# Chunked mLSTM with a gated MLP on one core: the state's part of the values computed in 64x64 tiles of the array, with the state and the scaled queries split by head half

## The chip, the cores and the metric

The kernel runs on one core of a Trainium2 chip. The metric is the device time of one execution in microseconds (us), taken as the median of several runs. The engines go by the profile's names: PE is the matrix unit (its weight loads are listed apart as PEld), DVE the vector engine, ACT the scalar engine, POOL the general-purpose engine, SP the queue that issues most transfers.

## The reference

A gated linear recurrence runs over 768 time steps for 4 x 8 = 32 batch-head pairs with head size 40; its output is regrouped into 3072 tokens of 320 features, and a two-layer MLP with a gate follows.

```python
for t in range(S):
    m_new = np.maximum(f_gate[:, :, t] + m, i_gate[:, :, t])
    f_stab = np.exp(f_gate[:, :, t] + m - m_new)
    i_stab = np.exp(i_gate[:, :, t] - m_new)
    C = f_stab[..., None, None] * C + i_stab[..., None, None] * einsum('bhd,bhe->bhde', vt, kt)
    n = f_stab[..., None] * n + i_stab[..., None] * kt
    h_tilde = einsum('bhde,bhe->bhd', C, qt);  denom = max(abs(n . qt), 1)
    y[:, :, t] = sigmoid(o_gate) * h_tilde / denom
x = y as (3072, 320)
h = x @ w_in;  g = h * sigmoid(h);  out = g @ w_out
```

## The kernel before

**Units.** The recurrence is computed in chunks of 64 steps (12 chunks, index c). The 32 batch-head pairs form two groups (index p) of 16 sequences. One chunk of one group is a unit, n = 2c + p, 24 in all. The 16 sequences of a unit are ordered by two batch halves and 8 heads; the code splits the 8 into two halves of four. In the kernel's indices d and a each stand for a half: a tile's rows hold one half (rows 0-39 and rows 64-103), its columns the other.

**What a unit does.** `scores` (L516) multiplies keys and queries in 64x64 tiles of the array. `weigh` (L550) multiplies the scores by the decay matrix `D`. `near_values` (L587) multiplies the weighted scores with the values of the same chunk, also in 64x64 tiles: 16 matmuls, four to a round over two row halves d and two column halves g. `far_values` (L604) adds what comes from the state of all chunks before: 8 matmuls that use all 104 rows of the scaled queries `qt` against the state `Cm`, whose tile holds two columns blocks per row, one of them zero (82 columns in all). `state` (L660) forms this chunk's contribution `pu`. `carry` (L677) decays the state on POOL (L688, by the last column of `lq`) and adds `pu` on DVE (L694). The scaled queries come from `near` (L506), one POOL multiplication of `q` and `lq`, 104 rows by 512, behind `look` (L503), the exponential of `lq` on ACT. The first three units use `values` (L566) in place of `near_values` and `far_values`.

**The MLP.** Three units give 384 tokens, a step j (8 steps). A step runs through 16 column blocks fc of the hidden layer: `mm1` (L763) makes `ph`, `act` makes `g` with ACT (L770) and DVE (L776 in step 0, L784 and L793 later), `mm2` (L814) adds the block of two fc earlier to the output. Steps after the first split each operand in a high and a low part and so take more matmuls.

**What sets the order.** All engines run orders written out by hand: the order of the calls. In step j the three units of step j + 1 are woven in. `PLACES` (L41) says at which fc each unit's block starts: 5, 9 and 12 in step 0 and 2, 7 and 12 later. At that fc `block` (L845) issues, behind `mm1`, the scores of the next unit, then `near_values`, `far_values` and `state` of this one. Two fc later (`2 in at`, L1062) `misc` of the next unit issues `look` on ACT and `near` on POOL. Unit 5, the last of the three woven into step 0, so has its `near` at fc 11 and its block at fc 12; all later units have two fc or more between them. Unit 5's output is normed and scaled by DVE behind the block (`norm`, `level`, `scale`), and `carry` follows.

PE works through its instructions in the order written; a matmul that waits holds back all behind it. The pair tile `p` has 8 heads x 128 columns: the scores in columns 0 to 63 of each head, the values from column 64 on. Every POOL or ACT instruction waits its turn in the same way. `qt`, `lq` have two buffers each.

Of the kernel before, what the change touches and what calls it, by code (L numbers as in the profile page):

```python
# [8 lines left out]
F32 = mybir.dt.float32  # L9
# [5 lines left out]
ALU = mybir.AluOpType  # L15
# [3 lines left out]
B, H, S, D = 4, 8, 768, 40  # L19
L = 64  # L20
NC = S // L
NP = B // 2
# [4 lines left out]
UPS = 3  # L27
# [3 lines left out]
D1 = D + 1  # L31
DA = 32
HD1 = H * D1
KS = 64 + D
# [9 lines left out]
def mlstm_mlp_kernel(  # L44
# [12 lines left out]
    nc = tc.nc  # L57
    pool = lambda n, b, **kw: ctx.enter_context(tc.tile_pool(name=n, bufs=b, **kw))
    cp = pool("cp", 1)
    p2 = pool("p2", 2)  # L60
# [19 lines left out]
    for k in range(2):  # L80
        m = mask[k * L : (k + 1) * L]
        nc.gpsimd.affine_select(
            out=m, in_=m, compare_op=ALU.is_ge, fill=NEG, base=0,
# [253 lines left out]
        nmade[0] = min(nmade[0] + n, len(parts))  # L337


    Cm = [cp.tile([KS, 2, HD1], F32, name=f"Cm{p}") for p in range(NP)]  # L340
    vb = [cp.tile([128, 2, HD1], F32, name=f"vb{k}") for k in range(3)]
    for t in vb:
        for k in range(2):
            nc.gpsimd.memset(t[k * L : (k + 1) * L, 1 - k, :], 0.0)
    for t in Cm:
        nc.gpsimd.memset(t, 0.0)

    def bank(n, pool_, tag, shape, name):

        if n < UPS:  # L350
            return pool_.tile(shape, F32, tag=tag, name=name)
        return psU.tile(shape, F32, tag="u", name=name)
# [5 lines left out]
    class Unit:  # L358
# [62 lines left out]
        def reach_act(self):  # L421
            self.lq = p2.tile([128, H, L], F32, tag="lq", name=f"lq{self.n}")
            nc.scalar.activation(self.lq[:KS], self.eq[:KS], AF.Exp)

        def load_d(self):
            n, c, p = self.n, self.c, self.p
            self.Dm = p3.tile([128, H, L], F32, tag="D", name=f"D{n}")
            for k in range(2):
                r = p * 2 * H + k * H
                nc.sync.dma_start(  # L430
                    self.Dm[k * L : (k + 1) * L],
                    LFd[c, r : r + H, :].unsqueeze(0).broadcast_to([L, H, L]),
                )
# [68 lines left out]

        def look(self):  # L503
            nc.scalar.activation(self.lq[:KS], self.lq[:KS], AF.Exp)  # L504

        def near(self):  # L506
            self.qt = p2.tile([KS, H, L], F32, tag="qt", name=f"qt{self.n}")
            nc.gpsimd.tensor_tensor(out=self.qt, in0=self.q[:KS], in1=self.lq[:KS], op=ALU.mult)  # L508

        def misc(self):  # L510
# [55 lines left out]
        def values(self):  # L566

            p, po = self.p, self.out
            ops = [(po[:, :, a, e, :], self.Dm, self.vt, a, e) for a in range(2) for e in range(2)]
            if self.c > 0:  # L570
                ops += [
                    (po[:, d, :, e, :], self.qt, Cm[p].rearrange("p a (h f) -> p a h f", f=D1), d, e)
                    for d in range(2)
                    for e in range(2)
                ]
            for i, (to, w, m, x, e) in enumerate(ops):
                for g in range(2):
                    j = x * 4 + e * 2 + g
                    nc.tensor.matmul(
                        to[g * L : (g + 1) * L],  # L580
                        w[:, j, :],
                        m[:, :, j, :],
                        start=(i == 0),
                        stop=(i == len(ops) - 1),
                    )
# [16 lines left out]
                            )  # L602

        def far_values(self):  # L604
            cm = Cm[self.p].rearrange("p a (h f) -> p a h f", f=D1)
            for d in range(2):
                for e in range(2):
                    for g in range(2):
                        j = d * 4 + e * 2 + g
                        nc.tensor.matmul(  # L610
                            self.out[g * L : (g + 1) * L, d, :, e, :],
                            self.qt[:, j, :],
                            cm[:, :, j, :],
                            start=False,
                            stop=True,
                            skip_group_check=True,
                        )

        def norm(self):
            n, po = self.n, self.po  # L620
# [39 lines left out]
        def state(self):  # L660
            n, c, p = self.n, self.c, self.p
            if c == NC - 1:
                return
            pu = bank(n, psO, "o", [128, H, D1], f"pu{n}")
            by_d = pu.rearrange("p (d j) f -> p j d f", d=2)
            for j in range(4):
                for a in range(2):
                    nc.tensor.matmul(  # L668
                        by_d[a * 64 : a * 64 + D, j],
                        self.kw[:, a * 4 + j, :],  # L670
                        self.vt[:, :, a * 4 + j, :],
                        start=True,
                        stop=True,
                    )
            self.pu = pu

        def carry(self, copy=nc.scalar.copy):  # L677
            n, c, p = self.n, self.c, self.p
            if c == NC - 1:
                return  # L680
            pu = self.pu
            for a in range(2):
                r = slice(a * 64, a * 64 + D)
                v = Cm[p][r, a, :].rearrange("p (h e) -> p h e", e=D1)
                if c == 0:
                    copy(v, pu[r])
                    continue
                nc.gpsimd.tensor_tensor(  # L688
                    out=v,
                    in0=v,  # L690
                    in1=self.lq[r, :, L - 1].unsqueeze(2).broadcast_to([D, H, D1]),
                    op=ALU.mult,
                )
                nc.vector.tensor_tensor(out=v, in0=v, in1=pu[r], op=ALU.add)  # L694

        def room(self, to=psH, tag="h"):
            n = self.n
# [210 lines left out]
    for _ in range(2):  # L908
        nc.tensor.matmul(
            dummy, ident, ident.unsqueeze(1).broadcast_to([128, 4, 128]), start=True, stop=True  # L910
        )
    two = gates(2 * L, 4 * L)
    near, far = spread(2 * L, 4 * L, nc.gpsimd), spread(4 * L, S, nc.gpsimd)
    late = [gates(4 * L, 8 * L), gates(8 * L, S)]
    widen()
# [75 lines left out]
            u2.carry(),  # L991
            run(5, two),
            run(1, near),
            u3.reach_act(),
        ),
# [3 lines left out]
            u3.weigh(),  # L999
            wmake(2),  # L1000
            run(2, near),
            u4.load_kvo(),
            u4.load_d(),
# [152 lines left out]
```

## Time and profile before

| what | value |
|---|---|
| median of 3 runs | 448.28 us (447.94 to 448.96) |
| the profiled execution's own time | 447.96 us |
| its span, first to last instruction | 446.2 us |
| ACT busy | 209.7 us (47%) |
| DVE busy | 270.8 us (61%) |
| POOL busy | 123.1 us (28%) |
| granted PE clock | 1.000 |

The page gives each engine's busy time, the chain of work that ended last and the costliest groups of instructions; the views of waits, of the chain by time and of the timeline in a window are answers of the same trace. A duration in the timeline is that of one instruction or, with "x16", of a run of them from the first start to the last end. Matmuls overlap, so what a stage costs PE is read from ends or starts of successive stages, never from the sum of durations. One fp32 matmul leaves two records: the 16 matmuls of `near_values` stand as x32, the 8 of `far_values` as x16.

### The profile page before, as it was taken

Reading aid. Unit: us, or ns where it says so; the run is one execution under the profiler, and the core shown is the slowest. Engines: PE = TensorE matmul, PEld = TensorE weight load, DVE = VectorE, ACT = ScalarE, POOL = GpSimd, SP = SyncE. Lnnn points to the kernel's source line nnn. Section 1 sums busy time; section 2 is a strip of 40 time slices with the busy share of each in tenths; the row PEclk is TensorE's granted clock in tenths of the full one; section 3 lists DMA queues with packets and bytes.
Section 4 is the critical chain, followed back from the end, with each engine's and each line's share of the span. In section 5 each row is a group of like instructions: output and inputs, shape, how many; then the busy total and the mean of one; then the engine's idle time right before and its main releaser. Section 6 shows DMA issues by size and latency. Waiting matters only on the chain.

```text
span 446.2 us, 11064 instructions
## 1 busy us (share of the span) xinstructions
PE 439.0 (98%) x4488; PEld 406.1 (91%) x4488; DVE 270.8 (61%) x595; ACT 209.7 (47%) x439; POOL 123.1 (28%) x134
## 2 busy tenths in 40 slices
PE   8899999999999999999999999999999999999996
PEld 4667667899999999999999999999999999999995
DVE  5888699477874664654664656646646555444442
ACT  7683956445745434435435344354344354334332
POOL 5834144133231431431341323314314220000000
PEclk9999999999999999999999999999999999999999
DMA  8999695251340631424421433406314100001001
GB/s 259 379 355 311 182 298 148 82 166 41 119 140 23 163 111 34 137 53 133 141 86 55 126 82 118 140 18 170 100 42 141 46 25 1 1 1 46 0 1 44
DMA packets 28691, 50.38 MB, mean 113 GB/s; under 512 B 3968, under 2 KB 15248, under 8 KB 28640
## 3 DMA queue, kind: packets, MB, share of 16 engines
q1 hardware_dynamic: 28288, 49.25, 36.2%
q8 instruction: 35, 0.57, 0.5%
q10 hardware_dynamic: 288, 0.34, 0.3%
q14 instruction: 16, 0.13, 0.1%
q0 software_dynamic: 64, 0.08, 0.1%
HBM read 45.65 MB, written 4.01 MB: 111 GB/s over the span
## 4 chain that ended last, share of the span: by engine, by line
PE 95%; DMA 3%; SPq 1%; ACT 1%; DVE 0%; issue 0%
PE ph L763 42%; PE pout L814 40%; PE p L610 3%; PE p L524 3%; PE pu L668 3%; PE p L595 2%; PE p L710 2%; DMA qk<-in_qk_dram 1%; DMA ko<-in_ko_dram 1%; PE pt L195 1%; SPq L459 0%; DVE wi L257 0%; SPq L439 0%; SPq L450 0%; ACT wri L255 0%
## 5 line engine op out<-in xcount | busy, mean ns | idle before, releaser
L770 ACT ACTIVATE th<-ph 128x384 f32<-128x384 f32 x128 | 62.4, 487 | 156.0 <-PE ph L763 154.9
L784 DVE SCALAR_TENSOR_TENSOR th<-th,ph 128x384 f32<-128x384 f32 x112 | 62.2, 555 | 89.2 <-ACT th L770 88.5
L763 PE MATMUL ph<-xh,wh 128*128 128x384 f32 x336 | 115.3, 343 | 0.0
L763 PE MATMUL ph<-xl,wh 128*128 128x384 f32 x336 | 113.7, 338 | 0.0
L814 PE MATMUL pout<-woh,gh 128*128 128x320 f32 x336 | 105.4, 314 | 0.0
L814 PE MATMUL pout<-woh,gl 128*128 128x320 f32 x336 | 103.9, 309 | 0.0
L814 PE MATMUL pout<-wol,gh 128*128 128x320 f32 x336 | 103.2, 307 | 0.0
L793 DVE TENSOR_TENSOR gl<-th,gh 128x384 fp32r<-128x384 f32 x112 | 65.6, 586 | 47.5 <-ACT gh L789 47.5
L789 ACT CAST gh<-th 128x384 fp32r<-128x384 f32 x112 | 57.5, 513 | 63.4 <-DVE th L784 62.8
L763 PE MATMUL ph<-xh,wl 128*128 128x384 f32 x224 | 75.9, 339 | 0.0
L814 PEld LDWEIGHTS pout<-woh,gh 128*128 128x128 f32 x336 | 63.0, 188 | 2.0
L763 PEld LDWEIGHTS ph<-xh,wh 128*128 128x128 f32 x336 | 63.1, 188 | 0.2
L763 PEld LDWEIGHTS ph<-xl,wh 128*128 128x128 f32 x336 | 63.1, 188 | 0.2
L814 PEld LDWEIGHTS pout<-woh,gl 128*128 128x128 f32 x336 | 63.0, 188 | 0.1
L814 PEld LDWEIGHTS pout<-wol,gh 128*128 128x128 f32 x336 | 63.1, 188 | 0.0
L688 POOL TENSOR_TENSOR Cm<-Cm,lq 40x328 f32<-40x328 f32 x40 | 30.4, 761 | 117.8 <-PE p L610 116.2
L508 POOL TENSOR_TENSOR qt<-qk,lq 104x512 f32<-104x512 f32 x22 | 28.9, 1314 | 121.6 <-ACT lq L504 109.0
L763 PEld LDWEIGHTS ph<-xh,wl 128*128 128x128 f32 x224 | 42.1, 188 | 0.0
L814 PE MATMUL pout<-wo,g 128*128 128x320 f32 x96 | 28.7, 435 | 0.0
L491 POOL TENSOR_TENSOR D<-D,am 128x512 f32<-128x512 f32 x20 | 25.8, 1290 | 4.8 <-DMA D<-LFd 3.3
L483 POOL TENSOR_TENSOR am<-mask,aT 128x512 f32<-128x512 f32 x20 | 24.1, 1206 | 6.6 <-DVE aT L205 5.2
L763 PE MATMUL ph<-x,wi 128*128 128x384 f32 x64 | 23.6, 492 | 1.3 <-DVE wi L257 1.3
(120 smaller groups left out, 488.1 us busy)
## 6 DMA issues: line engine op xcount, KB each, us to landing
qk<-in_qk_dram SPq DMA_DIRECT2D x24, 512.0 KB, 5.1
ko<-in_ko_dram SPq DMA_DIRECT2D x24, 320.0 KB, 4.7
wro<-in_w_out_dram SPq DMA_DIRECT2D x8, 640.0 KB, 7.2
D<-LFd SPq DMA_DIRECT2D x40, 128.0 KB, 3.4
lq<-LFd SPq DMA_DIRECT2D x40, 128.0 KB, 4.2
wri<-in_w_in_dram SPq DMA_DIRECT2D x8, 512.0 KB, 6.8
vb<-in_vp_dram SPq DMA_DIRECT2D x48, 82.0 KB, 4.6
out_dram<-ob SPq DMA_DIRECT2D x45, 80.0 KB, 2.1
```

What stands on the lines that cost most here:

```text
L483: nc.gpsimd.tensor_tensor(out=self.am, in0=mask.unsqueeze(1).broadcast_to([128, H, L]), in1=aT[:, self.c, self.p, :].unsqueeze(2).broadcas ...
L491: nc.gpsimd.tensor_tensor(out=self.Dm, in0=self.Dm, in1=self.am, op=ALU.add)
L508: nc.gpsimd.tensor_tensor(out=self.qt, in0=self.q[:KS], in1=self.lq[:KS], op=ALU.mult)
L524: nc.tensor.matmul(self.ps[d * L : (d + 1) * L, a * 4 + j, :], self.k[r, d * 4 + j, :], self.q[r, d * 4 + j, :], start=True, stop=True,)
L610: nc.tensor.matmul(self.out[g * L : (g + 1) * L, d, :, e, :], self.qt[:, j, :], cm[:, :, j, :], start=False, stop=True, skip_group_check=True,
L688: nc.gpsimd.tensor_tensor(out=v, in0=v, in1=self.lq[r, :, L - 1].unsqueeze(2).broadcast_to([D, H, D1]), op=ALU.mult,)
L763: nc.tensor.matmul(ph, w, x, start=(i == 0), stop=(i == len(ops) - 1))
L770: nc.scalar.activation(th, ph, AF.Tanh, scale=0.5)
L784: nc.vector.scalar_tensor_tensor(out=th, in0=th, scalar=1.0, in1=ph, op0=ALU.add, op1=ALU.mult)
L789: nc.scalar.copy(gh, th)
L793: nc.vector.tensor_tensor(out=gl, in0=th, in1=gh.bitcast(F32), op=ALU.subtract)
L814: nc.tensor.matmul(self.po[t], g[:, ts], w, start=(fc == 0 and i == 0), stop=(last and i == len(ops) - 1),)
```

## The change

The state is now kept with one head half on rows 0-39 and the other on rows 64-103, without the zero blocks (328 columns in place of 2 x 328). `far_values` issues 16 matmuls of 40 rows and 41 columns, in the same order of halves as `near_values`, in place of 8 matmuls of 104 rows and 82 columns. The scaled queries have to stand in the same layout, so `near` writes them in four quarters (40 rows by 256), two of which go from one row half to the other. The decay of the state has to stand there too: `decay` copies the last column of `lq` to a new tile `fl` in four small ACT copies behind `look`. `carry` decays with `fl` (still two POOL instructions of 40 by 328) and adds `pu` in four DVE instructions of 40 by 164 in place of two of 40 by 328. The first three units keep the old layout in `C0` and write the new one at their end; in the opening ACT and DVE copy or add the state in quarters too, and POOL clears one state tile in place of two.

```diff
-    Cm = [cp.tile([KS, 2, HD1], F32, name=f"Cm{p}") for p in range(NP)]
+    Cm = [cp.tile([KS, HD1], F32, name=f"Cm{p}") for p in range(NP)]
+    C0 = cp.tile([KS, 2, HD1], F32, name="C0")
...
-    for t in Cm:
-        nc.gpsimd.memset(t, 0.0)
+    nc.gpsimd.memset(C0, 0.0)
...
+        def decay(self):
+            if self.n < UPS:
+                return
+            self.fl = p2.tile([128, H], F32, tag="fl", name=f"fl{self.n}")
+            for d, a, r, w in self.turns():
+                nc.scalar.copy(self.fl[w, a * 4 : a * 4 + 4], self.lq[r, d * 4 : d * 4 + 4, L - 1])
+        @staticmethod
+        def turns():
+            rows = [slice(x * 64, x * 64 + D) for x in range(2)]
+            return [(d, a, rows[a], rows[d]) for d in range(2) for a in range(2)]
...
         def look(self):
             nc.scalar.activation(self.lq[:KS], self.lq[:KS], AF.Exp)
+            self.decay()
...
         def near(self):
             self.qt = p2.tile([KS, H, L], F32, tag="qt", name=f"qt{self.n}")
+            if self.n >= UPS:
+                for d, a, r, w in self.turns():
+                    nc.gpsimd.tensor_tensor(
+                        out=self.qt[w, a * 4 : a * 4 + 4, :],
+                        in0=self.q[r, d * 4 : d * 4 + 4, :],
+                        in1=self.lq[r, d * 4 : d * 4 + 4, :],
+                        op=ALU.mult,
+                    )
+                return
             nc.gpsimd.tensor_tensor(out=self.qt, in0=self.q[:KS], in1=self.lq[:KS], op=ALU.mult)
...
         def far_values(self):
-            cm = Cm[self.p].rearrange("p a (h f) -> p a h f", f=D1)
-            for d in range(2):
+            cm = Cm[self.p].rearrange("p (h f) -> p h f", f=D1)
+            for a in range(2):
                 for e in range(2):
-                    for g in range(2):
-                        j = d * 4 + e * 2 + g
-                        nc.tensor.matmul(
-                            self.out[g * L : (g + 1) * L, d, :, e, :],
-                            self.qt[:, j, :],
-                            cm[:, :, j, :],
...
+                    for d in range(2):
+                        r = slice(d * 64, d * 64 + D)
+                        for g in range(2):
+                            j = a * 4 + e * 2 + g
+                            nc.tensor.matmul(
+                                self.out[g * L : (g + 1) * L, d, a, e, :],
+                                self.qt[r, j, :],
+                                cm[r, j, :],
...
         def carry(self, copy=nc.scalar.copy):
...
+            for d in range(2):
+                w = slice(d * 64, d * 64 + D)
                 nc.gpsimd.tensor_tensor(
-                    out=v,
-                    in0=v,
-                    in1=self.lq[r, :, L - 1].unsqueeze(2).broadcast_to([D, H, D1]),
+                    out=new[w],
+                    in0=new[w],
+                    in1=self.fl[w].unsqueeze(2).broadcast_to([D, H, D1]),
                     op=ALU.mult,
                 )
-                nc.vector.tensor_tensor(out=v, in0=v, in1=pu[r], op=ALU.add)
+                for a in range(2):
+                    v = new[w, a * 4 : a * 4 + 4, :]
+                    nc.vector.tensor_tensor(
+                        out=v, in0=v, in1=self.pu[d][a * 64 : a * 64 + D], op=ALU.add
+                    )
```

Two places show how the instructions move. The first is PE at fc 12 of step 0, the block of unit 5 (p6 is the pair tile, D5 the weighted scores of unit 5, Cm1 the state of its group, qt5 its scaled queries). Before:

```order
L595 MATMUL p6_1035<-vb2_137,D5_690 64x41 [waits DMAHW7_49,DMAHW2_49]
L595 MATMUL p6_1035<-vb2_137,D5_690 64x41
L595 MATMUL p6_1035<-vb2_137,D5_690 64x41 [waits DMAHW3_49,DMAHW0_49]
L595 MATMUL p6_1035<-vb2_137,D5_690 64x41 x13
L610 MATMUL p6_1035<-Cm1_134,qt5_1009 64x2x41 [waits Pool_49]
L610 MATMUL p6_1035<-Cm1_134,qt5_1009 64x2x41 x7
L668 MATMUL pu5_1076<-vb2_137,kw5_845 40x2x41 x8
L814 MATMUL pout0_0_582<-wo5_990,g0_10_970 128x320 [waits DVE_49]
```

And with the change, from the last matmuls of `near_values` (now L621) on:

```order
L621 MATMUL p6_1085<-vb2_138,D5_704 64x41 x13
L639 MATMUL p6_1085<-Cm1_134,qt5_1056 64x41 [waits Pool_49]
L639 MATMUL p6_1085<-Cm1_134,qt5_1056 64x41
L639 MATMUL p6_1085<-Cm1_134,qt5_1056 64x41 [waits Pool_49]
L639 MATMUL p6_1085<-Cm1_134,qt5_1056 64x41 x7
L639 MATMUL p6_1085<-Cm1_134,qt5_1056 64x41 [waits Pool_49]
L639 MATMUL p6_1085<-Cm1_134,qt5_1056 64x41 x5
L697 MATMUL pu5_1134<-vb2_138,kw5_877 40x2x41 x8
L870 MATMUL pout0_0_596<-wo5_1032,g0_10_1012 128x320 [waits DVE_49]
```

Eight matmuls with one wait on POOL have become sixteen with three: the first, the third and the ninth wait, for the first, the third and the fourth quarter. The second place is POOL around unit 5's `near`, between the decay matrix of unit 6 (D6) and the decay of the state (Cm1). Before:

```order
L491 TENSOR_TENSOR D6_871<-D6_871,am6_978 128x512 [waits DMAHW5_49,DMAHW4_49,Pool_49]
L508 TENSOR_TENSOR qt5_1009<-qk5_693,lq5_788 104x512 [waits DMAHW6_49,DMAHW7_49,DMAHW1_49,Activation_49]
L688 TENSOR_TENSOR Cm1_134<-Cm1_134,lq5_788 40x328 [waits DVE_49,PE_49]
L688 TENSOR_TENSOR Cm1_134<-Cm1_134,lq5_788 40x328 [waits DVE_49,Pool_49]
L483 TENSOR_TENSOR am7_1130<-mask_93,aT_114 128x512 [waits Pool_49]
```

With the change:

```order
L507 TENSOR_TENSOR D6_903<-D6_903,am6_1020 128x512 [waits DMAHW5_49,DMAHW4_49,Pool_49]
L527 TENSOR_TENSOR qt5_1056<-qk5_707,lq5_812 40x256 [waits DMAHW6_49,DMAHW1_49,Activation_49]
L527 TENSOR_TENSOR qt5_1056<-qk5_707,lq5_812 40x256 [waits DMAHW7_49,Pool_49]
L527 TENSOR_TENSOR qt5_1056<-qk5_707,lq5_812 40x256 x2
L740 TENSOR_TENSOR Cm1_134<-Cm1_134,fl5_1051 40x328 [waits DVE_49,PE_49,Activation_49] x2
L499 TENSOR_TENSOR am7_1190<-mask_93,aT_114 128x512 [waits Pool_49]
```

One multiplication of 512 columns has become four of 256 in the same place; nothing is moved past it.

More of the change, by code (lines that the diff above doesn't have):

```diff
@@ L504, in look @@
             nc.scalar.activation(self.lq[:KS], self.lq[:KS], AF.Exp)
+            self.decay()
         def near(self):
             self.qt = p2.tile([KS, H, L], F32, tag="qt", name=f"qt{self.n}")
+            if self.n >= UPS:
[7 more added lines that the diff above has]
+                return
             nc.gpsimd.tensor_tensor(out=self.qt, in0=self.q[:KS], in1=self.lq[:KS], op=ALU.mult)
@@ L571, in values @@
                 ops += [
-                    (po[:, d, :, e, :], self.qt, Cm[p].rearrange("p a (h f) -> p a h f", f=D1), d, e)
+                    (po[:, d, :, e, :], self.qt, C0.rearrange("p a (h f) -> p a h f", f=D1), d, e)
                     for d in range(2)
@@ L604, in far_values @@
         def far_values(self):
-            cm = Cm[self.p].rearrange("p a (h f) -> p a h f", f=D1)
-            for d in range(2):
+            cm = Cm[self.p].rearrange("p (h f) -> p h f", f=D1)
+            for a in range(2):
                 for e in range(2):
-                    for g in range(2):
-                        j = d * 4 + e * 2 + g
-                        nc.tensor.matmul(
-                            self.out[g * L : (g + 1) * L, d, :, e, :],
-                            self.qt[:, j, :],
-                            cm[:, :, j, :],
[L614 to L617, printed above, removed]
+                    for d in range(2):
[6 more added lines that the diff above has]
+                                cm[r, j, :],
+                                start=False,
+                                stop=True,
+                                skip_group_check=True,
+                            )
         def norm(self):
@@ L674, in state @@
                     )
-            self.pu = pu
+            self.pu = [pu[:, d * 4 : d * 4 + 4, :] for d in range(2)]
         def carry(self, copy=nc.scalar.copy):
@@ L680, in carry @@
                 return
[L681 to L687, printed above, removed]
+            rows = lambda C: C.rearrange("p (h f) -> p h f", f=D1)
+            new = rows(Cm[p])
+            if n < UPS:
+                for a in range(2):
+                    r = slice(a * 64, a * 64 + D)
+                    v = rows(C0[:, a, :])[r]
+                    if n == 2:
+                        nc.gpsimd.tensor_tensor(
+                            out=v,
+                            in0=v,
+                            in1=self.lq[r, :, L - 1].unsqueeze(2).broadcast_to([D, H, D1]),
+                            op=ALU.mult,
+                        )
+                    for d in range(2):
+                        pu = self.pu[d][r]
+                        w = slice(d * 64, d * 64 + D)
+                        if n == 0:
+                            copy(v[:, d * 4 : d * 4 + 4, :], pu)
+                        elif n == 1:
+                            copy(new[w, a * 4 : a * 4 + 4, :], pu)
+                        else:
+                            nc.vector.tensor_tensor(
+                                out=new[w, a * 4 : a * 4 + 4, :],
+                                in0=v[:, d * 4 : d * 4 + 4, :],
+                                in1=pu,
+                                op=ALU.add,
+                            )
+                return
+            for d in range(2):
+                w = slice(d * 64, d * 64 + D)
                 nc.gpsimd.tensor_tensor(
-                    out=v,
-                    in0=v,
-                    in1=self.lq[r, :, L - 1].unsqueeze(2).broadcast_to([D, H, D1]),
+                    out=new[w],
+                    in0=new[w],
+                    in1=self.fl[w].unsqueeze(2).broadcast_to([D, H, D1]),
                     op=ALU.mult,
                 )
-                nc.vector.tensor_tensor(out=v, in0=v, in1=pu[r], op=ALU.add)
+                for a in range(2):
+                    v = new[w, a * 4 : a * 4 + 4, :]
+                    nc.vector.tensor_tensor(
+                        out=v, in0=v, in1=self.pu[d][a * 64 : a * 64 + D], op=ALU.add
+                    )
         def room(self, to=psH, tag="h"):
```

## The prediction

> **What bounds the kernel now.** I read the page first, then PE's waits, then the chain by time. A word on size: 0.2%, 0.9 us here, is about what a measurement of this kernel can tell from no change.
>
> ```profile
> PE 439.0 (98%) x4488; PEld 406.1 (91%) x4488; DVE 270.8 (61%) x595; ACT 209.7 (47%) x439; POOL 123.1 (28%) x134
> PE ph L763 42%; PE pout L814 40%; PE p L610 3%; PE p L524 3%; PE pu L668 3%; PE p L595 2%; PE p L710 2%; DMA qk<-in_qk_dram 1%; DMA ko<-in_ko_dram 1%; PE pt L195 1%; SPq L459 0%; DVE wi L257 0%; SPq L439 0%; SPq L450 0%; ACT wri L255 0%
> ...
> PE dummy L909 <- POOL ident masks.py:199: 1.4, 1, 1.4
> PE ph L763 <- DVE wi L257: 1.3, 1, 1.3
> PE p L524 <- DVE D L551: 0.2, 1, 0.2
> PE po L579 <- issue: 0.2, 1, 0.2
> ```
>
> The second line is the chain that ended last: after the first 20 us it is PE alone. The four rows below are all that PE waited for, 3.1 us, all in the opening. So what shortens PE's stream shortens the run one for one, and any new wait of PE lengthens it one for one. `far_values` (L610) is 3% of the chain, the only stage that the change shortens.
>
> **What `far_values` costs and what replaces it.** The chain around the block of unit 13 (start, length, stage), then the last unit's, then two rows of PE's timeline from the opening.
>
> ```profile
> 211.59 0.62 PE p L524 x32
> 212.22 0.45 PE p L595 x32
> 212.66 0.72 PE p L610 x16
> 213.38 0.57 PE pu L668 x16
> 213.95 0.35 PE pout L814
> ...
> 384.95 0.72 PE p L610 x16
> 385.67 0.34 PE pout L814
> ...
> 12.03 0.69 PE L524 MATMUL p<-qk 40*64 40x64 f32 x32 [0.17 <-DVE D L551]
> 12.65 0.77 PE L668 MATMUL pu<-vb,kw 128*40 128x82 f32 x16
> ```
>
> These pieces run from the end of one stage to the end of the next. L668 follows L610 with as many records of the same 82 columns and takes 0.57; L610 itself takes 0.72, 0.15 more, and it is the one that follows a stage in 64x64 tiles. I read the 0.15 as the change of tile shape. In the opening L668 comes straight behind L524, which is in 64x64 tiles: ends at 12.72 and 13.42, so 0.70, a change of shape of 0.13.
>
> The new `far_values` has the records of `near_values` (L595): 32, of 64 weight columns and 41 moving ones, in the same order of halves, with 40 rows in place of 64 as L524 has them. No change of shape lies between the two any more; it moves behind `far_values`. I price it at 0.46: 0.45 by L595, and a little for L595's position behind a stage that loads the same way. A unit with `state` then takes 0.45 + 0.46 + 0.70 = 1.61 in place of 0.45 + 0.72 + 0.57 = 1.74: **0.13 less, 19 times (units 3 to 21), 2.5 us**. The last two units have no `state`; `pout` takes 0.34 behind L610 and 0.35 behind L668, so I let it cost the same behind 64x64 tiles: 0.72 - 0.46 = 0.26 less, twice, 0.5 us. **Sum 3.0.** Bounds: 3.2 with 0.45 throughout; 2.6 with a change of shape of 0.15 ahead of `state`; 1.7 if the new stage takes 0.50.
>
> **What the quarters cost.** `near` becomes four POOL instructions of 40 x 256. The trace has none of this shape. The nearest rows:
>
> ```profile
> L508 POOL TENSOR_TENSOR qt<-qk,lq 104x512 f32<-104x512 f32 x22 | 28.9, 1314 | 121.6 <-ACT lq L504 109.0 <-DMA vb<-in_vp_dram 5.4 <-DMA lq<-LFd 5.4
> L651 POOL TENSOR_TENSOR x<-ko,y 128x256 f32<-128x256 f32 x1 | 0.7, 738 | 0.1
> L688 POOL TENSOR_TENSOR Cm<-Cm,lq 40x328 f32<-40x328 f32 x40 | 30.4, 761 | 117.8 <-PE p L610 116.2
> L280 POOL TENSOR_TENSOR wh<-wtc,wh x2: 725/896/1066, 18.7 to 19.5; 64x256 fp32r<-64x256 f32 x2
> 2.87 2.40 POOL L344 MEMSET vb<- 64x328 f32 x6
> ```
>
> Columns set the time, not rows: 738 ns for 256 columns on 128 rows, 761 for 328 on 40. L280 writes to the other row half, as two of the quarters do, and takes 725 once and 1066 once (DVE was working in both). L344's six fills alternate between the row halves and still come 0.40 apart, so halves do not run side by side there. A quarter is thus at least half of L508, 0.65, and at most 1.07, nearest to 0.74.
>
> In most units this is covered. In unit 13 `near` starts at 206.63 and `far_values` at 212.6; even 4 x 1.07 = 4.3 fits in 6.0. Unit 5 is another matter, since its `near` comes one fc before its block:
>
> ```profile
> 66.10 1.30 POOL L508 TENSOR_TENSOR qt<-qk,lq 104x512 f32<-104x512 f32 x1 [6.09 <-ACT lq L504]
> 66.86 0.63 PE L595 MATMUL p<-vb,D 64*64 64x41 f32 x32
> 67.45 0.79 PE L610 MATMUL p<-Cm,qt 104*64 104x82 f32 x16
> L688 POOL TENSOR_TENSOR Cm<-Cm,lq 40x328 f32<-40x328 f32 x2 | 1.6, 816 | 1.0 <-PE p L610 0.9
> ...
> 206.63 1.30 POOL L508 TENSOR_TENSOR qt<-qk,lq 104x512 f32<-104x512 f32 x1 [5.44 <-ACT lq L504]
> ...
> 51.02 1.30 POOL L508 TENSOR_TENSOR qt<-qk,lq 104x512 f32<-104x512 f32 x1 [7.54 <-ACT lq L504]
> 54.21 0.63 PE L595 MATMUL p<-vb,D 64*64 64x41 f32 x32
> ```
>
> Unit 5's `qt` is done at 67.40 and `far_values` starts at 67.45: it fits by a hair today. With quarters of q each the fourth ends at 66.10 + 4q. PE would reach the ninth matmul, which needs it, at 66.86 + 0.45 + half of 0.46 = 67.54. PE waits 66.10 + 4q + 0.05 - 67.54 = **4q - 1.39**. For q I take 0.79: L651's 0.74, times 816/761, by which L688 was longer in the stretch from 61 to 72 us, where DVE is busy. That gives a wait of **1.8 us** (1.2 at q = 0.65, 2.9 at 1.07). Unit 4 has more room: 51.02 + 4q + 0.05 against 54.21 + 0.68 - 0.13, a wait only from q = 0.92, 0.6 at 1.07. Queued behind unit 5's waiting matmuls is all of PE: `state`, `mm2` of fc 10 and `mm1` of fc 13; nothing on PE makes the time good later. On POOL the state's decay waits for `far_values` anyway.
>
> **Small instructions elsewhere.** ACT gains four copies of 40 x 4 per unit; DVE four additions of 164 columns for two of 328; both also work in quarters in the opening.
>
> ```profile
> 9.47 0.20 ACT L535 COPY last<-D 128x8 f32<-128x8 f32 x1
> 9.58 0.59 ACT L394 ACTIVATE D<-e 128x512 f32<-128x512 f32 x1
> ...
> 67.07 0.47 ACT L770 ACTIVATE th<-ph 128x384 f32<-128x384 f32 x1
> ...
> 69.36 0.53 DVE L776 SCALAR_TENSOR_TENSOR g<-th,ph 128x384 f32<-128x384 f32 x1
> ...
> L655 DVE SCALAR_TENSOR_TENSOR x<-ko,p 128x256 f32<-128x256 f32 x21 | 8.8, 421 | 0.7
> L655 DVE SCALAR_TENSOR_TENSOR x<-ko,p 128x64 f32<-128x64 f32 x42 | 7.2, 214 | 0.0
> ...
> 27.08 0.28 DVE L180 TENSOR_TENSOR home<-home 32x128 f32<-32x128 f32 x1
> ...
> 28.38 0.85 PE L195 MATMUL pt<-ident,home 32*128 32x32 f32 x6
> ...
> 16.18 0.47 ACT L497 ACTIVATE ko<-ko 128x320 f32<-128x320 f32 x1 [1.33 <-DMA ko<-in_ko_dram]
> ```
>
> A copy of 8 columns takes 0.20 on ACT and the next instruction starts 0.11 behind it: 0.5 to 0.8 us per unit. Behind unit 5's copies stands `th` of fc 12 at 67.07; moved to 67.9 it still ends ahead of DVE's `g` at 69.36, which waits for DVE's own queue. On DVE two rows of L655 give 1.08 ns per column and 145 fixed, so 164 columns take 0.32 and four 1.3, 0.3 more than today. In the opening that falls twice between 24.7 and 26.8 and moves L180's end from 27.36 to about 28.0, ahead of PE's L195 at 28.38: covered by 0.4, and if that cover goes, each 0.1 us more costs PE as much. ACT's quarter copies of the first state lie ahead of a wait of 1.33 for a transfer. I cost all of this at nothing. POOL's dropped fill lies in idle time.
>
> **Sum.** -3.0 + 1.8 = -1.2 us. Against the profiled execution, 447.96, that is 446.8. It lies 0.3 below the median of three, 448.28, of which I take the change: **447.1 us**.
>
> **The rivals.**
>
> *The quarters overlap on POOL* (0.10). Quarters that stand on different rows would run side by side, the four in the time of two: 66.10 + 1.58, and unit 5 waits 0.2. The run gains 2.8, 445.5. Against it stand L344's fills on alternating halves, 0.40 apart at 0.37 each. [...]
>
> *A quarter costs nearly what the whole did* (0.07), the slower end. If a POOL instruction's time hangs little on its columns, q is up to 1.30: unit 5 waits 3.8 and unit 4 waits 51.02 + 5.2 + 0.05 - 54.76 = 1.5, together 5.3 against 3.0, a time of 450.6. The two waits together exceed 3.0 from q = 1.01 and cost 0.9 more than that from q = 1.12. For it speaks L280's 1066, against it L651.
>
> *The row halves of the new `far_values` take turns* (0.03). The stage would cost 2 x 0.45 = 0.90, a unit 0.45 + 0.90 + 0.70 = 2.05, so 19 x 0.31 + 2 x 0.18 = 6.3 lost, and with unit 5's wait (shorter by the later arrival, 1.5) 456. Against it: each half d goes to four heads of `p` of its own, as in `near_values`, and L595 shows no turns. [...]
>
> *A second wait of 0.5 to 1.5 us in step 0* (0.08): DVE or ACT late by the small instructions, or unit 4's quarters at 0.95. The time is 447.6 to 448.6.
>
> **How the numbers follow.** The forecast itself has 0.72. Within it q of 0.65 to 0.95 and the bounds of 3.0 spread the time over 446.2 to 448.0, two thirds of it more than 0.9 below 448.28: 0.47 faster, 0.25 within. With the rivals: faster 0.47 + 0.10 = 0.57, within 0.25 + 0.08 = 0.33, slower 0.07 + 0.03 = 0.10. The range 445.6 to 448.8 takes in the forecast, the second wait, q up to 1.07, and leaves out the overlap and both slow cases.
>
> **What would show it.** In the changed profile, the chain's piece for `far_values` at 0.46 and for `state` at 0.70, with 32 records in the first; one new wait of PE on `qt` in unit 5, near 67.5 us, of 1.2 to 2.9; POOL's quarters at 0.65 to 1.07; all other stages as before. I am wrong if the first piece exceeds 0.55, if unit 5's wait is missing or over 3, or if PE waits anywhere else after 30 us.

## The result and the profile after

| | median, us | runs | profiled execution | its span | granted PE clock in it |
|---|---|---|---|---|---|
| before, measured beside the change | 449.78 (447.94 to 452.77) | 16 | | | |
| with the change | 452.41 (450.70 to 454.38) | 16 | 454.38 | 452.6 | 0.992 |

The ratio is 1.0051, 95% interval [1.0026, 1.0075]: **slower, by 2.6 us between the medians**, where 1.2 faster was predicted. The page of the changed kernel, its busy times and the line of PE's clock:

```profile
PE 440.9 (97%) x4824; PEld 406.3 (90%) x4824; DVE 284.9 (63%) x637; ACT 226.6 (50%) x525; POOL 159.7 (35%) x196
...
PEclk9999998989999999999999999999999999999999
```

ACT, DVE and POOL work more, as the change says. New is the clock that PE is granted: two of the 40 slices show 8 in place of 9, between 68 and 102 us. All 16 runs show a mean of 0.991 to 0.995. The waits of PE (what waited, for what: us in total, times, longest):

```profile
PE p L639 <- POOL qt L527: 2.2, 3, 1.3
PE ph L819 <- DVE wi L257: 1.4, 1, 1.4
PE dummy L965 <- POOL ident masks.py:199: 1.4, 1, 1.4
...
PE p L766 <- DVE x L684: 0.6, 1, 0.6
...
PE pout L870 <- DVE Cm L731: 0.3, 1, 0.3
```

The first is unit 5's wait for the quarters. `p L766 <- x` is unit 4's transpose, which waits for its scaled output, in step 0 too; `pout <- Cm` is in the opening. None of these three stood in the waits of before. The wait for `wi` did (1.3). Four more, 1.7 in all (for a transfer, for `D`, for `kw` and of `px`), lie in the first 20 us.

**The gain is there.** The chain around a steady block of the changed kernel (start, length, stage):

```profile
98.85 0.62 PE p L550 x32
99.47 0.45 PE p L621 x32
99.92 0.47 PE p L639 x32
100.39 0.70 PE pu L697 x16
```

`far_values` (L639) takes 0.47, `state` (L697) 0.70, together with `near_values` (L621) 1.62 in place of 1.74. **The loss is in step 0.** PE's timeline from the block of unit 5 on, then POOL's:

```profile
69.06 0.63 PE L621 MATMUL p<-vb,D 64*64 64x41 f32 x32
69.96 0.31 PE L639 MATMUL p<-Cm,qt 40*64 40x41 f32 x4 [0.27 <-POOL qt L527]
71.54 0.44 PE L639 MATMUL p<-Cm,qt 40*64 40x41 f32 x16 [1.27 <-POOL qt L527]
72.69 0.43 PE L639 MATMUL p<-Cm,qt 40*64 40x41 f32 x12 [0.70 <-POOL qt L527]
73.05 0.77 PE L697 MATMUL pu<-vb,kw 128*40 128x82 f32 x16
73.74 3.57 PE L870 MATMUL pout<-wo,g 128*128 128x320 f32 x6
77.11 1.18 PE L819 MATMUL ph<-x,wi 128*128 128x384 f32 x3
```

```profile
69.04 3.60 POOL L527 TENSOR_TENSOR qt<-qk,lq 40x256 f32<-40x256 f32 x4 [5.98 <-ACT lq L520]
```

The same place in the kernel before:

```profile
68.07 0.74 PE L668 MATMUL pu<-vb,kw 128*40 128x82 f32 x16
68.74 1.88 PE L814 MATMUL pout<-wo,g 128*128 128x320 f32 x6
70.46 1.45 PE L763 MATMUL ph<-x,wi 128*128 128x384 f32 x4
```

From the start of `near_values` to that of `state` PE takes 73.05 - 69.06 = 3.99; before it took 68.07 - 66.86 = 1.21. Then `pout` of fc 10 takes 77.11 - 73.74 = 3.37 up to the next stage, where it took 70.46 - 68.74 = 1.72 before. It waits for nothing there; its clock is cut. Windows of the changed kernel (us, then busy time of PE, PEld, DVE, ACT, POOL, then the granted clock, the DMA share and GB/s):

```profile
73.50:74.00 0.50, 0.50 (x11) 0.39 (x6) 0.50 (x3) 0.00 (x0) 0.50 (x1) 0.78 0.07 27
74.00:77.00 3.00, 3.00 (x6) 1.93 (x7) 2.81 (x11) 0.00 (x0) 2.77 (x4) 0.50 0.33 102
77.00:77.50 0.50, 0.50 (x3) 0.26 (x2) 0.47 (x3) 0.00 (x0) 0.50 (x2) 0.81 0.05 16
77.50:78.00 0.50, 0.50 (x3) 0.35 (x2) 0.47 (x2) 0.00 (x0) 0.50 (x1) 1.00 0.00 0
```

Half clock for 0.22 + 3.00 + 0.19 = 3.41 us, and full again. At half the clock that is 1.7 us of work lost, right behind the wait. A second stretch of this kind lies behind the last `pt` stage, 18 small matmuls (L195) in a row:

```profile
85.00:90.00 5.00, 5.00 (x31) 4.03 (x30) 1.95 (x5) 1.95 (x7) 3.23 (x4) 1.00 0.13 45
90.00:95.00 5.00, 5.00 (x18) 3.83 (x17) 2.01 (x4) 1.62 (x3) 0.00 (x0) 0.66 0.00 0
```

### The profile page after: what moved, and what is told of

It reads as the page before. It is cut to its first block, busy times and chain, and to the rows that moved or that the text cites. A ratio compares the mean times of both kernels' runs of the same rounds, so it can differ in the third digit from the quotient of the medians.

```text
span 452.6 us, 11901 instructions
## 1 busy us (share of the span) xinstructions
PE 440.9 (97%) x4824; PEld 406.3 (90%) x4824; DVE 284.9 (63%) x637; ACT 226.6 (50%) x525; POOL 159.7 (35%) x196
## 4 chain that ended last, share of the span: by engine, by line
PE 83%; POOL 0%; DVE 0%; issue 0%
PE pout L870 37%; PE ph L819 36%; PE pu L697 3%; PE p L550 2%; PE p L639 2%; PE p L621 2%; PE p L766 1%; PE pt L195 0%; POOL qt L527 0%; DVE ob L888 0%
## 5 line engine op out<-in xcount | busy, mean ns | idle before, releaser
L527 POOL TENSOR_TENSOR qt<-qk,lq 40x256 f32<-40x256 f32 x84 | 63.8, 759 | 126.3 <-ACT lq L520 120.7
L849 DVE TENSOR_TENSOR gl<-th,gh 128x384 fp32r<-128x384 f32 x112 | 74.4, 664 | 47.5 <-ACT gh L845 47.5
L740 POOL TENSOR_TENSOR Cm<-Cm,fl 40x328 f32<-40x328 f32 x38 | 29.2, 770 | 81.4 <-PE p L639 79.4
L870 PE MATMUL pout<-wo,g 128*128 128x320 f32 x96 | 32.3, 475 | 0.3 <-DVE Cm L731 0.3
L870 PEld LDWEIGHTS pout<-wo,g 128*128 128x128 f32 x96 | 19.3, 207 | 6.9 <-issue 2.3
```

The source lines that it names most:

```text
L527: nc.gpsimd.tensor_tensor(out=self.qt[w, a * 4 : a * 4 + 4, :], in0=self.q[r, d * 4 : d * 4 + 4, :], in1=self.lq[r, d * 4 : d * 4 + 4, :], ...
L740: nc.gpsimd.tensor_tensor(out=new[w], in0=new[w], in1=self.fl[w].unsqueeze(2).broadcast_to([D, H, D1]), op=ALU.mult,)
L849: nc.vector.tensor_tensor(out=gl, in0=th, in1=gh.bitcast(F32), op=ALU.subtract)
L870: nc.tensor.matmul(self.po[t], g[:, ts], w, start=(fc == 0 and i == 0), stop=(last and i == len(ops) - 1),)
```

## The experiments

Each was timed in turns with the kernel before; the first four, the next four and the last three each shared a chip and the runs of before. Theory A is unit 5's wait with the half clock behind it, B is that the clock falls by chance of phase; C is that slower DVE and ACT spread the loss over step 0.

| label | what | median, us | before | ratio [95%] |
|---|---|---|---|---|
| a0_after | the change again | 453.15 | 448.34 | 1.0091 [1.0059, 1.0123] |
| e1_early | unit 5's `misc` one fc earlier | 449.26 | 448.34 | 1.0003 [0.9972, 1.0034] |
| e2_warm | matmuls of no use in unit 5's wait | 450.92 | 448.34 | 1.0054 [1.0032, 1.0077] |
| e3_before_late | before, unit 5's `near` three times | 453.95 | 448.34 | 1.0109 [1.0055, 1.0164] |
| e4_loaded | `qt`, `lq` loaded in the new order | 446.79 | 448.66 | 0.9970 [0.9936, 1.0003] |
| e5_copies | e4 with the ACT copies | 448.25 | 448.66 | 0.9982 [0.9956, 1.0007] |
| e6_quarters | e4 with the POOL quarters | 451.31 | 448.66 | 1.0064 [1.0036, 1.0092] |
| e7_before_split | before, `pt` stage in two | 447.48 | 448.66 | 0.9987 [0.9968, 1.0007] |
| e8_loaded_split | e4 with e7's split | 445.98 | 448.51 | 0.9950 [0.9931, 0.9970] |
| e9_carry_first | e8, opening reordered | **445.37** | 448.51 | **0.9931 [0.9911, 0.9952]** |
| e10_after_split | the change, `pt` stage in two | 452.37 | 448.51 | 1.0094 [1.0066, 1.0123] |

**The change again**, as the reference for the three behind it.

> The changed kernel itself, on the same chip as the next three. All theories: 0.3 to 0.7% slower than before, about 2.3 us. Theory A (unit 5's wait for the quarters, and the half clock that follows it) expects in every profile a wait of PE of 2.0 to 2.8 us near 70 us and a stretch of 3.4 us at a clock of 0.5 right behind it. Theory B (the clock falls by chance of phase, not for the wait) expects the stretch in some profiles only, or elsewhere.

The ratio, 0.9% slower, is above the 0.3 to 0.7% expected; its interval and that of the first measurement overlap. All seven runs show a granted clock between 0.988 and 0.995, as Theory A has it and B does not. In its profile PE waits 2.0 for `qt`; the window 70 to 75 us has the clock at 0.62 and 75 to 80 at 0.70, two half-clock stretches in a row, and there is none behind `pt`. The first begins at 71.2, while PE still waits for the fourth quarter (until 72.4).

**Unit 5's `near` earlier.**

```diff
-                units[at[2].n + 1].misc()
+                if at[2].n != 4:
+                    units[at[2].n + 1].misc()
...
+                if at[1].n == 4:
+                    units[5].misc()
```

> The changed kernel with unit 5's gate, exponential, decay copies and quarters issued at fc 10 of step 0, behind unit 4's transpose, in place of fc 11. Theory A: the wait and the half clock at 70 us both go, 3.5 to 4.5 us less than the changed kernel, 0.2 to 0.5% faster than before. Theory B: only the wait goes, 2.0 to 2.6 us less, level with before. Theory C (the loss is spread over step 0 by slower DVE and ACT): under 1 us less.

3.9 us less than a0_after, so level with the kernel before, where A had it 0.2 to 0.5% faster. From the waits of PE in its profile:

```profile
PE p L766 <- DVE x L684: 1.5, 2, 1.0
```

No wait on `qt`, and no half clock near 70 us in this profile, though seven of the ten runs show a granted clock of 0.992 to 0.996. What stays are the waits on `x`, one more than in the change: 0.54 at unit 4's transpose, and 0.99 at unit 5's, ahead of which DVE's scan takes 1.22 and `kw` 1.25, where they took 0.67 and 0.96 in the kernel before. What share of the wait they make was not followed. So A holds for most of the loss, and C for a rest.

**Matmuls of no use in the gap.** Ten matmuls of 328 columns stand between `near_values` and `far_values` of unit 5; nothing reads what they write.

```diff
         u.near_values()
+        if n == 5:
+            u.pu_tile = bank(n, psO, "o", [128, H, D1], f"pu{n}")
+            warm(10, u.pu_tile)
         u.far_values()
```

> The changed kernel with ten matmuls of no use (328 columns, written to the tile that state overwrites) between unit 5's near_values and far_values, some 1.5 us of PE work inside the wait. Theory A: unit 5's far_values end as late as before or at most 0.3 us later, the half clock behind them goes, 1.3 to 1.7 us less than the changed kernel. Theory B: no change, or up to 0.3 us more, with a half clock somewhere as often as without them.

2.2 us less than a0_after, somewhat more than the 1.3 to 1.7 expected. PE's own wait is down to 0.7, since the added work fills the rest, and the clock stays up behind it (first row below, 68 to 73 us; second row 73 to 78), while `pt` is followed by a half clock in this profile (third row):

```profile
68.00:73.00 5.00, 4.31 (x82) 3.10 (x74) 4.24 (x7) 3.35 (x7) 4.17 (x6) 1.00 0.90 258
73.00:78.00 5.00, 5.00 (x22) 3.50 (x21) 4.69 (x16) 1.30 (x3) 3.31 (x4) 1.00 0.22 56
85.00:90.00 5.00, 5.00 (x25) 4.12 (x25) 1.91 (x5) 1.62 (x3) 0.36 (x1) 0.76 0.00 0
```

The late `qt` is as late as before (done 3.43 us behind the start of PE's `near_values`, 3.58 in the change); that the run is shorter with more work on PE is the clock. This speaks against B.

**A wait in the kernel before**, with nothing else of the change.

```diff
-            nc.gpsimd.tensor_tensor(out=self.qt, in0=self.q[:KS], in1=self.lq[:KS], op=ALU.mult)
+            for _ in range(3 if self.n == 5 else 1):
+                nc.gpsimd.tensor_tensor(out=self.qt, in0=self.q[:KS], in1=self.lq[:KS], op=ALU.mult)
```

> The kernel before with unit 5's scaled queries computed three times over (same result), so that they are done 2.6 us later and nothing else of the change is there. Theory A: PE waits 2.5 to 2.7 us at 67 us, a half clock of 3.4 us follows that costs 1.7, 4.0 to 4.5 us more than before (0.9 to 1.0%). Theory B: 2.5 us more (0.6%), full clock behind the wait.

5.6 us more than the kernel before, for a wait of 3.3; both are above what Theory A expected. Its windows:

```profile
65.00:70.00 5.00, 1.90 (x68) 1.39 (x66) 4.42 (x6) 3.31 (x6) 4.33 (x3) 0.88 0.91 258
70.00:80.00 10.00, 9.84 (x56) 7.24 (x57) 7.37 (x17) 1.46 (x4) 4.46 (x6) 0.72 0.15 51
```

(1 - 0.88) x 5 + (1 - 0.72) x 10 = 3.4 us of clock are lost, two stretches of 3.4 us at half in a row. They begin near 68.8, while PE still waits (until 70.2), so that part of them costs nothing. A wait alone does it, in the old layout too.

**The layout without its by-products.** A second copy of `q` is loaded straight into `qt` in the new order, and `lq` too. `near` is one POOL instruction of 104 x 512 again, and the decay needs no copies.

```diff
-                    "(d a e) t -> a d (e t)", d=2, a=2
+                    "(d a e) t -> d a (e t)", d=2, a=2
...
+        def load_qt(self):
+            self.qt = p2.tile([KS, H, L], F32, tag="qt", name=f"qt{n}")
+            src = qk[n].rearrange("(a k) x -> k a x", a=2)
+            for d in range(2):
+                m = 64 if d == 0 else D
+                nc.sync.dma_start(
+                    self.qt[d * 64 : d * 64 + m].rearrange("p (a e) t -> p a (e t)", a=2),
+                    src[:m, :, d * 4 * L : (d + 1) * 4 * L],
+                )
...
+                nc.gpsimd.tensor_tensor(out=self.qt, in0=self.qt, in1=self.lq[:KS], op=ALU.mult)
```

> The change with its two by-products taken away: lq and a second copy of q are loaded straight into the order by half d (two more transfers of q per unit), so qt is one POOL multiplication of 104 x 512 again and no copies of 40 x 4 are needed on ACT; PE's stages and DVE's four additions stay as in the change. Theory A with C (the loss is all by-products: the wait for the quarters with the half clock behind it, and the lateness by copies and quarters): no wait of PE on qt, no half clock near 70 us, no waits on x; only the opening's +0.5 and the gain of 0.13 per unit stay, so 0.5 - 3.2 = -2.7 against the kernel before, a median near 445.6 (ratio 0.994). Rival D (DVE's four additions alone make x late, the +0.76 at fc 10): still a wait on x of 0.5 to 1.0, 446.4. Theory B (the half clock falls by chance of phase, whatever waits): a stretch of 3.4 us at half clock between 65 and 80 us here too, 447 or more.

Its waits of PE, without the first and the last, which every profile here has:

```profile
PE ph L822 <- DVE wi L257: 1.2, 1, 1.2
PE pout L873 <- DVE Cm L734: 0.2, 1, 0.2
```

Neither `qt` nor `x` any more; DVE's four additions alone (rival D) don't make `x` late. Three runs at a granted clock of 1.0 took 444.33 to 445.15, no slower than A with C has it; the other seven show 0.989 to 0.996 and 446.3 to 450.7. So the median is 1.2 above what was expected, and the interval just reaches 1. That low clock remained to be explained.

**The copies alone, the quarters alone**, each on top of e4_loaded.

```diff
+                nc.scalar.copy(self.fl[w, a * 4 : a * 4 + 4], self.lq[w, a * 4 : a * 4 + 4, L - 1])
```

> As e4_loaded, with the four copies of 40 x 4 on ACT put back (qt stays one multiplication). If the copies are what makes DVE and unit 5's near late (C by ACT): wi on DVE comes some 0.8 later in units 4 and 5, x of unit 4 late by 0.3 to 0.7, unit 5's near 0.5 to 0.8 later than the kernel before against a slack of 0.05, so PE waits 0.5 to 0.8 for qt; in all 1 to 1.5 above e4_loaded. If the quarters on POOL are what does it (C by POOL): as e4_loaded within 0.4.

```diff
+                for d, a, r, w in self.turns():
+                    h = slice(a * 4, a * 4 + 4)
+                    nc.gpsimd.tensor_tensor(
+                        out=self.qt[w, h, :], in0=self.qt[w, h, :], in1=self.lq[w, h, :], op=ALU.mult
+                    )
```

> As e4_loaded, with qt in four quarters on POOL and no copies on ACT: the term of the prediction by itself. The prediction as made: quarters of 0.79, unit 5's near where it was, PE waits 1.8 for qt and nothing follows: e4_loaded + 1.8. Theory A: the same wait, 1.8 to 2.3, and behind it 3.4 us at half clock, 1.7 more: e4_loaded + 3.5 to 4.0. If the copies are needed for the loss: a wait under 1.2 and no half clock, e4_loaded + 0.5 to 1.2.

With the copies alone the median is 1.5 above e4_loaded, at the top of what was expected; PE waits 0.8 on `qt`, and the clock from 60 us on is 1.00. With the quarters alone it is 4.5 above, more than any theory had. POOL's timeline in unit 5 of e6_quarters, PE's, then its windows:

```profile
67.53 3.68 POOL L536 TENSOR_TENSOR qt<-qt,lq 40x256 f32<-40x256 f32 x4 [6.53 <-ACT lq L529]
```

```profile
67.57 0.63 PE L628 MATMUL p<-vb,D 64*64 64x41 f32 x32
...
70.20 0.44 PE L646 MATMUL p<-Cm,qt 40*64 40x41 f32 x16 [1.57 <-POOL qt L536]
71.27 0.43 PE L646 MATMUL p<-Cm,qt 40*64 40x41 f32 x12 [0.63 <-POOL qt L536]
71.63 0.77 PE L704 MATMUL pu<-vb,kw 128*40 128x82 f32 x16
```

```profile
72.00:73.00 1.00, 1.00 (x13) 0.71 (x8) 0.93 (x4) 0.00 (x0) 0.93 (x2) 0.67 0.08 16
73.00:74.00 1.00, 1.00 (x3) 0.68 (x2) 0.90 (x4) 0.00 (x0) 0.92 (x2) 0.50 0.00 0
```

The wait and the half clock are both there without any copies. And POOL starts only 0.04 ahead of PE's `near_values`, where it had a lead of 0.76 in the kernel before (66.10 against 66.86). In e5_copies, where PE waits 0.8 on `qt`, that lead is as short. Either by-product alone takes the lead away; there they don't add up.

**How the lead is lost.** DVE's timeline in unit 4 of the changed kernel, then ACT's behind it, then three of these rows in e4_loaded, which has neither by-product:

```profile
54.66 0.78 DVE L257 SCALAR_TENSOR_TENSOR wi<-wri 128x512 uint32<-128x512 uint32 x1 [1.96 <-ACT wri L256]
55.36 1.23 DVE L175 TENSOR_TENSOR_SCAN home<-home 32x256 f32<-32x256 f32 x1
```

```profile
64.85 0.83 ACT L278 CAST wh<-wtc 64x256 fp32r<-64x256 f32 x2 [0.62 <-DVE wtc L257]
...
68.34 0.62 ACT L520 ACTIVATE lq<-lq 104x512 f32<-104x512 f32 x1
68.99 0.83 ACT L434 COPY fl<-lq 40x4 f32<-40x4 f32 x4
```

```profile
52.15 0.76 DVE L257 SCALAR_TENSOR_TENSOR wi<-wri 128x512 uint32<-128x512 uint32 x1 [0.97 <-ACT wri L256]
52.81 0.67 DVE L175 TENSOR_TENSOR_SCAN home<-home 32x256 f32<-32x256 f32 x1
```

```profile
61.85 0.83 ACT L278 CAST wh<-wtc 64x256 fp32r<-64x256 f32 x2
```

ACT's four copies (0.83) stand ahead of `wri`, and DVE waits 1.96 for it (0.97 in e4_loaded and in the kernel before). POOL's quarters run beside DVE's scan, which takes 1.23 in place of 0.67: it takes 1.21 to 1.23 in all six profiles that have quarters and 0.67 in the seven that have none. Either way DVE is late through unit 4, ACT waits 0.62 for `wtc` (in e5_copies and e6_quarters too), and `lq` of unit 5 stands behind that in ACT's queue. At unit 4's `x`, PE takes 1.94 from `pout` to the next `mm1` in e4_loaded, 2.09 with the copies alone, 2.30 with the quarters alone and 2.72 with both, in the change. Why the scan takes longer beside the quarters is not shown.

**The second half clock.** The kernel before shows a granted clock under 0.998 in 31 of the 74 runs timed here, most of them 0.994 or 0.996. A stretch of 3.41 us at half in 446 gives 0.996.

```diff
+            if c == (c0 + c1) // 2 - 1 and lo == 4 * L:
+                yield
...
-        14: lambda: units[8].load(),
+        14: lambda: (units[8].load(), run(1, far)),
```

> The kernel before, with the 18 small matmuls of the last pt stage in two groups of 9 that stand one fc apart. Theory P (the half clock that some runs show behind this stage comes from its 2.2 us of small matmuls in a row): no run with a granted clock under 0.998, the upper runs (449 to 453) gone, median 447.7. Rival (those runs have their low clock from elsewhere or by chance): the same spread as the kernel before, about a third of the runs under 0.998, ratio 1.000.

None of its ten runs is under 0.998, and the upper runs are gone (447.21 to 448.95). The median is 1.2 lower; the interval of the ratio just reaches 1.

**The split in e4_loaded**, with the same edit.

> e4_loaded with the last pt stage in two groups of 9 small matmuls one fc apart, as in e7_before_split. Theory P (7 of e4_loaded's 10 runs were under a granted clock of 0.998 because of that stage): no run under 0.998 now, all runs where e4_loaded's three at full clock were, 444.3 to 446, median 445.0, ratio against the kernel before 0.992. Rival (the low clock has another source): median 446.8 as e4_loaded, runs of 0.996 and less remain.

Eleven of twelve runs are at 0.998 or above, one at 0.995. The median is 445.98, not the 445.0 expected; the best run is 445.19.

**The opening's additions earlier**, on top of e8_loaded_split.

```diff
-            wmake(1),
             u1.carry(nc.vector.tensor_copy),
+            wmake(1),
             u2.carry(),
```

> e8_loaded_split with the copies of u1's first state ahead of wo on DVE in the opening (they fill the 0.79 us in which DVE waits for ACT). If the +0.49 at fc 2 is PE waiting in pout for the PSUM bank that u2's four additions free: the additions end 0.7 earlier, the wait goes, e8_loaded_split - 0.4 to 0.5, 444.6. If it is something else in the opening: no change against e8_loaded_split, or slower where wo now comes too late for the first pout.

0.6 less than e8_loaded_split, and `pout <- Cm` is gone from PE's waits: the opening's loss (0.2 in e8_loaded_split's waits) was the PSUM bank (one of the three buffers of the pool `psO`) that `u2`'s four additions free. The ratios' intervals of the two overlap, so the 0.6 itself is not certain. Two of its twelve runs are at 0.991 and 0.994; in the profile, one of them, the clock is low in the opening (0.83 from 0 to 20 us), where PE waits 1.0 for a transfer, and 1.00 behind `pt`. This version is faster than the kernel before, 0.9931 [0.9911, 0.9952], by 3.1 us. The split alone took the kernel before down by 1.2, so an estimate of 2 is left for the layout and the new order of the opening.

**The split in the change**, with nothing else.

> The change as it is, with only the pt stage split. Theory A with P: the wait of 2 us in unit 5 and the half clock right behind it stay, a second half clock at the pt stage goes: granted clocks of 0.992 to 0.996 in all runs, median 451.9 (a0_after had 453.15), ratio 1.008. Rival (one cause for all low clocks, the pt stage): clock 1.0 in most runs, 450.

452.37 against 453.15 of a0_after, which was timed beside another set of runs of before, and four runs only: the clocks are 0.991 to 0.996. In its profile PE waits 2.2 for `qt`, the window 70 to 75 us is at 0.71, and 85 to 95 us at 1.00. So in this profile the split takes away the one behind `pt`, and the one behind unit 5's wait stays. The other three runs, at 0.991 to 0.994, lost more clock than one such stretch; none of them was profiled.

## Why the prediction was wrong

**The gain was right.** 0.47 and 0.70 were forecast as 0.46 and 0.70, with 32 records. The change of tile shape went where it was put. One bound was added up wrong: with 0.50 for the new stage the gain is 19 x 0.09 + 2 x 0.22 = 2.2, not 1.7. In e4_loaded, where little covers it, PE runs up 3.1 us from fc 2 of step 0 to the end (0.13 a unit, 0.25 for each of the last two), against the 3.0 of the sum.

**The term of unit 5's wait was mis-sized: 1.8 was forecast, 4.6 came.** It has four parts, from the rows above:

| part | us |
|---|---|
| as predicted, q = 0.79 | 1.8 |
| q is 3.60 / 4 = 0.90, so 4q - 1.39 = 2.2 | + 0.4 |
| `near` starts 0.02 ahead of PE's `near_values`, not 0.76 | + 0.7 |
| half clock behind the wait: `pout` 3.37 in place of 1.72 | + 1.65 |
| sum | 4.6 |

Check: 3.99 + 3.37 - 1.21 - 1.72 = 4.4, and the 0.13 that unit 5 gains is in it. The wait itself, 2.2 in the view, lies in the forecast's 1.2 to 2.9, for the matmuls of the first quarters run inside it; what it cost does not. (The prediction and the text ahead of it have the ninth matmul wait for the fourth quarter. It is the eleventh: the `order` rows count 10 ahead of it, the timeline 4 + 16 records. That takes 0.06 off each of the prediction's waits of unit 5.)

The first step that failed is "I cost all of this at nothing". It stands for the 0.7 of the lost lead here, and for 0.8 and 0.5 more below. The covers for ACT's copies were read for `th` of fc 12 and for the opening only. The rows that stand between unit 4's copies and unit 5's `lq`, over `wri`, DVE, `wtc` and back to ACT, were not followed; that DVE's scan takes 1.23 in place of 0.67 beside POOL's quarters was not counted at all. The second is the price of the wait, "nothing on PE makes the time good later": true, but a wait of PE can cost more than its length, here 1.65 more. The trace of before had the clock at 1.000 throughout, and I took the price of a wait as its length.

**Two covers gave way beside it.** In the opening DVE's eight small instructions (1.34 and 1.33 in the changed kernel, 1.00 and 1.02 before) take 0.65 longer, as forecast (0.6). But the cover named, that of L195 on L180, was not the first to go: the third `pout` waits for the bank that the additions free (shown as 0.26), and fc 2 comes 0.5 late. The other is unit 4's `x`. PE's timeline of the changed kernel around its transpose, then that of before:

```profile
60.84 1.78 PE L870 MATMUL pout<-wo,g 128*128 128x320 f32 x6
63.17 0.55 PE L766 MATMUL p<-ident,x 128*128 128x128 f32 x3 [0.56 <-DVE x L684]
63.56 1.46 PE L819 MATMUL ph<-x,wi 128*128 128x384 f32 x4
```

```profile
59.41 1.78 PE L814 MATMUL pout<-wo,g 128*128 128x320 f32 x6
61.03 0.49 PE L710 MATMUL p<-ident,x 128*128 128x128 f32 x3
61.35 1.46 PE L763 MATMUL ph<-x,wi 128*128 128x384 f32 x4
```

From `pout` to the next `mm1` it is 2.72 in place of 1.94, so 0.8 for a wait shown as 0.56. This is the rival "a second wait of 0.5 to 1.5 us in step 0"; it came on top of the forecast, not in its place, and it is the sign of being wrong that the prediction named, a wait elsewhere after 30 us.

The sum by what the runs showed is -3.1 + 4.6 + 0.5 + 0.8 = **+2.8**. The medians differ by 2.6, with an interval of 1.2 to 3.4; timed again as a0_after it was 4.1, 2.6 to 5.5, so the closeness to 2.6 is in part luck. The two profiled executions differ by 6.4. By the starts of their `mm1`, 1.2 of this lies ahead of fc 2, 0.5 at fc 2, 0.8 at unit 4's `x`, 4.6 at unit 5 and 1.7 behind `pt`; the gain comes to 2.4 there, 0.7 less than in e4_loaded, and what takes the 0.7 was not followed.

**The other rivals fell.** The quarters don't overlap (3.60 for four; a quarter's median in the trace is 0.73, the longest 1.21). The row halves don't take turns (0.47). A quarter doesn't cost the whole.

**What stays open.** The half clock comes with a wait of 2.0 to 3.3 us in all five profiles that have one, and not with one of 0.7 or 0.8 (e2_warm, e5_copies); no run tried a length between. The traces say a little more. Within each of them the clock changes only on a grid with a step of 3.41 us: in the changed kernel the second stretch begins 17.1 us, five steps, behind the first. The step of this grid ahead of the first stretch, then the step of e2_warm that holds most of its wait (columns as in the windows above):

```profile
70.36:73.78 3.42, 1.53 (x45) 1.25 (x45) 2.69 (x4) 2.41 (x5) 2.74 (x4) 1.00 0.90 268
70.53:73.94 3.41, 2.79 (x35) 2.16 (x36) 3.27 (x8) 0.88 (x2) 2.71 (x4) 1.00 0.71 203
```

In the five profiles with the long wait PE is busy for 1.35 to 1.96 us of the step after which the clock falls from 1.00; between 60 and 76 us every step with 2.43 or more is followed by full clock, unless the clock had fallen already. In the opening busy time alone doesn't tell: a step with 1.78 was followed by a fall (e5_copies), one with 1.83 was not (the changed kernel). The grid lies differently in each execution (a step ends at 73.78 in the changed kernel and at 73.94 in e2_warm), and this may be why the kernel before loses its clock behind `pt` in some runs only. Of the nine profiles with the whole stage, five have 2.10 us or more of its 2.19 within one step, and four of these lose the clock behind it; of the four with 2.04 or less none does. No run moved the grid, so this is not shown. With the `pt` stage split, 31 of 34 runs without a late `qt` are at full clock; of the other three only one was profiled.

## What to carry to other kernels

Price a new wait of the matrix engine with what its clock does behind it: here 2.2 us of waits were followed by 1.7 us of lost clock, and a wait of 2.0 came with two such stretches (a0_after). Idle time of an engine is no cover by itself: ACT is busy for 50% of the span here, and behind its copies of 0.83 DVE waits 1.96 for `wri` in place of 0.97. Follow the queue of the engine that gets the new instruction to the next thing that the bound engine reads, one unit further than the one that was changed. When a layout changes, look first whether the transfer can write the new one: here two more transfers per unit took the place of four copies on ACT and of three more instructions on POOL, and kept the gain.

## What the hardware showed that was not expected

- PE's granted clock falls to 0.50 for 3.41 us, or twice that, with a wait of 2.0 to 3.3 us, even where some matmuls run inside the wait: in the five profiles with such a wait PE was busy for 1.35 to 1.96 us (40 to 57%) of the 3.41 us ahead of the fall.
- A stage of 18 matmuls of 32 columns without any wait (2.19 us) can be followed by the same fall, as in four profiles here (the changed kernel, e2_warm, e3_before_late, e6_quarters): 31 of 74 runs of the kernel before show a low clock, 3 of 34 in the kernels that split the stage and have no late `qt`.
- Four POOL instructions of 40 x 256, two for each row half, take 3.60 us, one after another, and a scan on DVE beside such four takes 1.23 us in place of 0.67.
